# A three-stage kernel: the first stage's on-chip pools in another order, two pool ends aligned, and the stage's last stores issued by GpSimd

## The chip, the cores and the metric

The kernel runs on one core of one Trainium2 chip. The metric is the device time of one execution in microseconds (us). Before the change the median of three runs is 4724.49 us (4724.1 to 4726.25).

## What is computed

The reference is a forward pass and its gradients. With `x` of 2048 rows by 640 columns:

```python
xn = layernorm(x)
s  = A(xn, mem0, Wq, Wk, Wv, Wo)   # 64 segments of 32 rows, 32 heads of 128; 8 memory rows are carried on
g  = silu(B(xn, w1, w3, w2))       # B: (silu(xn w1) * (xn w3)) w2, hidden width 1728
out = x + s * g
# and the gradients of x, mem0, Wq, Wk, Wv, Wo, w1, w3, w2 for a given grad_out
```

Branch A is recurrent: each segment attends over 8 memory rows and its own 32 rows, and the first 8 rows of its result are the next segment's memory. Branch B is a gated feed-forward layer without recurrence. All tensors are bf16.

## The kernel before, in words

The work runs as a row of stages. Each stage opens its own tile pools in on-chip memory (SBUF) and in the matmul result banks (PSUM). Pools are laid out one behind the other in the order in which they are opened, and when a stage closes its pools the next stage's pools take the same addresses. The first instruction that touches a tile of a new pool waits until the old pools that this new pool overlaps have been left: by the engines that read or wrote their tiles, and by the transfers out of them.

**Stage one** (`phase12_ln_Bfwd`, L1809) normalizes the rows of `x`, stores them to the scratch tensor `XN`, and runs branch B forward in four blocks of 512 rows (`hidden`, L1868; `up`, L1900). It opens four SBUF pools in the order `bw` (the weights w1s, w3s, w2s, 52,480 bytes of a partition), `bio` (`hBT` and `xnT_b`), `bwork` (temporaries, among them `gb`, `dz`, `gs`), `ln` (the row tiles `xt0` to `xt7`). At its end (L1991 to L1999) it projects the first 672 rows of `XN` with Wv: 20 units of `first_rows` (L357) and one `last_rows` (L374), with the last block's four `up` calls in between, in units n = 1, 4, 7 and 10. A `first_rows` unit is ten matmuls in two halves; DVE copies the first half out of PSUM and ACT the second (L90, L92), into staging tiles `b0st` that take turns in the eight slots `xt0` to `xt7`, and each half is stored to the scratch tensor `QVX` by a DMA that SyncE (SP) issues (L371, L386): 42 stores in all.

**Stage two** (`phase3_Afwd`, L389) opens pool `W4` with Wq and Wo, pool `ast` with kT0, kT1, vt, hx0, hx1 and smaller tiles, and then calls `first_part` (L412). This opens `b0` (the turned rows `b0x`, and `ride0` and `kr0`) and `b0s` (four staging tiles of 1024 columns). Its work on the engines is: SP loads `b0x` as six turned blocks of 112 rows out of `XN` and then `ride0` (L270, called from L422 and L449); GpSimd (POOL) clears hx0 and hx1 (L427) and copies `ride0` into hx0 (L450). PE turns six heads of Wv (L444, called from L465), with each result copied into a ring in kT1 and stored to `WVT` by SP (L447). Then 42 units run (L468 to L495): `first_rows` and `last_rows` for Wk, then for Wq. ACT's queue issues the nine loads of Wq and Wo between them (L472), POOL stores the units up to n = 35 (to `KX` and `QVX`) and SP the rest.

**The recurrence** (`recurrence`, L555) opens `achain` and `afill` where `b0` and `b0s` lay and runs `chain(t)` (L598) 64 times. One step starts with two half projections by Wk, whose results DVE copies to the tile `stg` (L606); the next half, by Wq, goes into the bank that the first copy must have emptied. SP issues the step's stores and loads in the order in which they stand, `ride` (L572) among them.

The order within each engine's queue is the order in which instructions stand in the built program; `in_order` (L273) ties them. An instruction that waits holds back all that stand behind it on its engine.

In bytes of a partition, the old layout puts `bw` at 99,200 to 151,680, `bio` at 151,680 to 190,592, `bwork` at 190,592 to 218,880 and `ln` at 218,880 to 229,248. Stage two puts Wq and Wo at 99,200 to 181,120, `ast` at 181,120 to 211,456, `b0` at 211,456 to 220,224 and `b0s` from 220,224 on. The recurrence puts `achain` at 211,456 to 220,384.

Of the kernel before, what the change touches and what calls it, by code (L numbers as in the profile page):

```python
# [9 lines left out]
BF16 = mybir.dt.bfloat16  # L10
# [6 lines left out]
P = 128  # L17
# [255 lines left out]
def in_order(k, start):  # L273

    tc = k.tc
    last = {}
    for ins in tc.nc.cur_bb.bb.instructions[start:]:
        p = last.get(ins.engine)
        if p is not None:
            tc.add_manual_dep(ins, p.name, mybir.DependencyInfo(mybir.DependencyClass.NoSync, mybir.DependencyReason.DATA),  # L280
                              reason="written order")
        last[ins.engine] = ins
# [18 lines left out]
def packed_half(k, bank, x, W, b):  # L301

    for dc in range(k.DC):
        for g in range(4):
            c0 = g * 1024 + b * 512
            k.nc.tensor.matmul(bank[32 * g:32 * g + 32, :], x[:, dc, :], W[:, dc, c0:c0 + 512],  # L306
                               start=(dc == 0), stop=(dc == k.DC - 1), tile_position=(0, 32 * g),
                               skip_group_check=True)
# [48 lines left out]
def first_rows(k, ps, stage, xs, off, W, dst, x0, cg, tag="b0pb", w=1024, q=None):  # L357

    nc = k.nc
    for b in range(2):  # L360
        c0 = cg * 1024 + b * 512
        if w == 512 or b == 0:
            st = stage()
        pb = ps.tile([P, 512], F32, name="b0pb", tag=tag if isinstance(tag, str) else tag[b])
        for dc in range(k.DC):
            nc.tensor.matmul(pb[:], xs[:, dc, x0 - off:x0 - off + P], W[:, dc, c0:c0 + 512],
                             start=(dc == 0), stop=(dc == k.DC - 1))
        s0 = b * 512 if w == 1024 else 0
        k.copy(st[:, s0:s0 + 512], pb[:], eng='vs'[b])
        if w == 512 or b == 1:  # L370
            (q or nc.sync).dma_start(dst[x0:x0 + P, cg * 1024 + (b * 512 if w == 512 else 0):cg * 1024 + b * 512 + 512], st[:])  # L371


def last_rows(k, ps, stage, xs, off, W, dst, tag="b0pb", w=1024, q=None):  # L374

    x0 = k.NB0 - 32
    for b in range(2):
        if w == 512 or b == 0:
            st = stage()
        pb = ps.tile([P, 512], F32, name="b0pb", tag=tag if isinstance(tag, str) else tag[b])  # L380
        packed_half(k, pb, xs[:, :, x0 - off:x0 - off + 32], W, b)
        s0 = b * 512 if w == 1024 else 0
        k.copy(st[:, s0:s0 + 512], pb[:], eng='vs'[b])
        if w == 512 or b == 1:
            c0, c1 = (b * 512 if w == 512 else 0), b * 512 + 512
            (q or k.nc.sync).dma_start(dst[x0:k.NB0].rearrange("r (g c) -> g r c", g=4)[:, :, c0:c1], st[:])  # L386


def phase3_Afwd(k, W0, W4, Wv, Wk_, out2):  # L389
    nc, tc = k.nc, k.tc  # L390
    D, DC, S, H, HD, T = k.D, k.DC, k.S, k.H, k.HD, k.T
    Wq = W4.tile([P, DC, HD], BF16, name="Wq", tag="w2")
    Wo = W4.tile([P, H, D], BF16, name="Wo", tag="w3")
    with tc.tile_pool(name="ast", bufs=1) as st:
        kTs = [st.tile([P, H, 120], BF16, name=f"kT{i}") for i in range(2)]

        vt = st.tile([P, HD // 2], BF16, name="vt")
        hxs = [st.tile([P, DC, 32], BF16, name=f"hx{i}") for i in range(2)]
        qTs = [st.tile([P, 4, P], BF16, name=f"xqT{i}") for i in range(3)]
        xPs = [st.tile([P, 4, P], BF16, name=f"xP{i}") for i in range(3)]  # L400
        PTs = [st.tile([P, 4, P], BF16, name=f"xPT{i}") for i in range(2)]
        oTm = st.tile([P, H, 32], BF16, name="oTm")
        first_part(k, Wv, Wk_, Wq, Wo, kTs, vt, hxs, qTs + xPs + PTs + [oTm])
        with tc.tile_pool(name="aps", bufs=1, space=bass.MemoryType.PSUM) as ps, \
                tc.tile_pool(name="apm", bufs=1, space=bass.MemoryType.PSUM) as psm:
            banks = [psm.tile([P, 512], F32, name=f"bank{i}") for i in range(3)]
            own = kTs, vt, hxs, qTs, xPs, PTs, oTm
            WT = recurrence(k, W0, W4, Wv, Wk_, Wq, Wo, own, ps, banks)
            phase4_Abwd(k, out2, W4, WT, own, ps, banks)


def first_part(k, Wv, Wk_, Wq, Wo, kTs, vt, hxs, rest):  # L412
    nc, tc = k.nc, k.tc
    DC, H, HD = k.DC, k.H, k.HD
    with tc.tile_pool(name="b0", bufs=1) as io, tc.tile_pool(name="b0s", bufs=4) as stp, \
# [1 line left out]
            tc.tile_pool(name="b0k", bufs=2, space=bass.MemoryType.PSUM) as pk, \  # L417
            tc.tile_pool(name="b0w", bufs=2, space=bass.MemoryType.PSUM) as pw:
        start = len(nc.cur_bb.bb.instructions)
        xs = io.tile([P, DC, k.NB0], BF16, name="b0x")  # L420
        for x0 in range(0, k.NB0, 112):
            turned_load(k, xs[:, :, x0:x0 + 112], k.XN[x0:x0 + 112, :])  # L422
        wq = k.A_Wq.rearrange("(dc p) h e -> p dc (h e)", p=P)
# [43 lines left out]
        n = 0  # L467
        for W, dst in ((Wk_, k.KX[:, :]), (Wq, k.QVX[:, 0])):  # L468
            for x0 in list(range(0, k.NB0 - 32, P)) + [None]:
                for cg in range(4 if x0 is not None else 1):  # L470
                    if n % 2 == 1 and fetch:
                        nc.scalar.dma_start(*fetch.pop(0))  # L472
                    stage = lambda: stp.tile([P, 1024], BF16, name="b0st", tag="b0st")
# [1335 lines left out]
def phase12_ln_Bfwd(k: K, Wv, Wk_):  # L1809
    nc, tc = k.nc, k.tc  # L1810
    D, DC, S, F, FC, NT = k.D, k.DC, k.S, k.F, k.FC, k.NT
    BLK = 512
    NBLK = S // BLK
    TB = BLK // P
    fszs = [min(P, F - fc * P) for fc in range(FC)]
    with tc.tile_pool(name="bw", bufs=1) as wp, tc.tile_pool(name="bio", bufs=2) as io, \
            tc.tile_pool(name="bwork", bufs=2) as wk, tc.tile_pool(name="ln", bufs=1) as ln, \
            tc.tile_pool(name="bps", bufs=2, space=bass.MemoryType.PSUM) as ps:
        start = len(nc.cur_bb.bb.instructions)
        w1s = wp.tile([P, DC, F], BF16, name="w1s")  # L1820
# [73 lines left out]
        def up_ld(blk, ti):  # L1894
            tt = TB * blk + ti
            Gt = wk.tile([P, D], BF16, name="Gt", tag="Gt")
            nc.sync.dma_start(Gt[:], k.G[tt * P:(tt + 1) * P, :])
            gts[tt] = Gt

        def up(blk, ti):  # L1900
            hBT = hBTs[blk % 2]
            tt = TB * blk + ti
            rows = slice(tt * P, (tt + 1) * P)
            pz = ps.tile([P, 2, 512], F32, name="pz", tag="pz")
            for i in range(2):
                for fc in range(FC):
                    nc.tensor.matmul(pz[:, i, 0:320], hBT[:, fc, ti * P:(ti + 1) * P],
                                     w2s[:, fc, 320 * i:320 * i + 320], start=(fc == 0), stop=(fc == FC - 1))
            halves = lambda t: t[:].rearrange("p (i c) -> p i c", i=2)
            sz = wk.tile([P, D], BF16, name="sz", tag="sz")  # L1910
            nc.scalar.activation(halves(sz), pz[:, :, 0:320], ACT.Sigmoid)
            gb = wk.tile([P, D], BF16, name="gb", tag="gb")
            nc.vector.tensor_tensor(halves(gb), pz[:, :, 0:320], halves(sz), ALU.mult)
            nc.gpsimd.dma_start(k.GB[rows, :], gb[:])
            dz = wk.tile([P, D], BF16, name="dz", tag="dz")
            nc.scalar.activation(halves(dz), pz[:, :, 0:320], ACT.Sigmoid, scale=-1.0)
            nc.vector.tensor_tensor(dz[:], dz[:], gb[:], ALU.mult)
            nc.vector.tensor_tensor(dz[:], sz[:], dz[:], ALU.add)
            nc.gpsimd.dma_start(k.DZ[rows, :], dz[:])
            gs = wk.tile([P, D], BF16, name="gs", tag="gs")  # L1920
            nc.vector.tensor_tensor(gs[:], gts.pop(tt)[:], gb[:], ALU.mult)
            nc.gpsimd.dma_start(k.GS[rows, :], gs[:])
# [58 lines left out]
        xb = io.tile([P, DC, BLK], BF16, name="xnT_b", tag="xnT_b")  # L1981
# [3 lines left out]
        xa, off = xnTs[NBLK], 0  # L1985
# [5 lines left out]
        for n, (x0, cg) in enumerate([(x0, cg) for x0 in range(0, k.NB0 - 32, P) for cg in range(4)]):  # L1991
            if n % 3 == 1 and n // 3 < TB:
                up(NBLK - 1, n // 3)
                if n < 6:
                    up_ld(NBLK - 1, n // 3 + 2)
            if x0 == BLK:
                xa, off = xb, BLK
            first_rows(k, ps, stage, xa, off, Wv, k.QVX[:, 1], x0, cg, tag=("pg", "pu"), w=512)
        last_rows(k, ps, stage, xb, BLK, Wv, k.QVX[:, 1], tag=("pg", "pu"), w=512)  # L1999
        in_order(k, start)  # L2000


# [191 lines left out]
def kernel(  # L2194
# [34 lines left out]
    with tc.tile_pool(name="W0", bufs=1) as W0:  # L2229
        Wv, Wk_ = [W0.tile([P, k.DC, k.HD], BF16, name=nm, tag=tag) for nm, tag in (("Wv", "w0"), ("Wk", "w1"))]  # L2230
        phase12_ln_Bfwd(k, Wv, Wk_)
        with tc.tile_pool(name="W4", bufs=1) as W4:
            phase3_Afwd(k, W0, W4, Wv, Wk_, out_2)
# [38 lines left out]
```

## Time and profile before

| what | value |
|---|---|
| median of three runs | 4724.49 us |
| profiled execution, its time | 4722.13 us |
| profiled execution, its span from first to last instruction | 4720.1 us |
| PE (matmuls) busy | 4476.3 us, 95% |
| DVE, ACT, POOL busy | 48%, 34%, 44% |
| mean granted PE clock | 0.985 of full |
| PE in the last 12 us of stage one (250 to 262 us) | busy 12.00 of 12.00 us |
| PE from 262 to 272 us | busy 2.66 of 10.00 us |
| PE from 376.0 to 384.3 us | busy 2.87 of 8.30 us |
| DMA engines from 276 to 340 us | 98% and 101% of their time in the two parts of it |

The profile tells for each engine what it did and when (the timeline), with idle time ahead of an instruction in square brackets and the name of what ended that idle time. The granted clock is the share of full speed that the matmul engine was allowed in that stretch. Times count from the start of the span. "SPq" or "ACTq" marks the queue of an engine issuing a DMA; the time beside it is the issue alone and not the transfer.

### The profile page before, as it was taken

To read this page: it belongs to the slowest core of one execution; us is meant where nothing else is said; L and a number is where in the kernel's file an instruction comes from. 1 tells how busy PE (TensorE), PEld (TensorE's weight loads), DVE (VectorE), ACT (ScalarE), POOL (GpSimd) and SP (SyncE) were. 2 spreads that over 40 slices of the span, in tenths; PEclk is the share of its full clock that TensorE was granted. 3 is DMA by queue.
4 is the path that set the end of the run, shared out by engine and by line. 5 is a ranking of instruction groups with operands and counts; after the bars stand their busy time and mean duration, and the time that the engine had idled before them with its cause. 6 is when DMAs were issued, how large, how long until landed. Compare 5 with 4: busy or idle time off the path is not lost. (4 is left out here: it accounts for less than half of the span.)

```text
span 4720.1 us, 160254 instructions
## 1 busy us (share of the span) xinstructions
PE 4476.3 (95%) x64504; PEld 2824.1 (60%) x64504; DVE 2244.0 (48%) x7156; ACT 1588.8 (34%) x4360; POOL 2093.8 (44%) x3514
## 2 busy tenths in 40 slices
PE   8998999999999888999999998999999999999999
PEld 4544555555555555666666665666567666666675
DVE  8734666666666534555555553343234332311460
ACT  5432555555544533333333332232223322200000
POOL 6522555555555423444444444454345533311340
PEclk9998999999999998999999998999999999999999
DMA  8773666666555678777777774754345543579673
GB/s 265 238 244 106 176 182 179 177 180 178 175 174 167 169 179 230 208 215 203 212 210 213 205 210 133 163 150 133 109 125 157 145 125 109 170 219 208 154 183 100
DMA packets 977976, 834.81 MB, mean 177 GB/s; under 512 B 518674, under 2 KB 859862, under 8 KB 975272
## 3 DMA queue, kind: packets, MB, share of 16 engines
q1 hardware_dynamic: 765871, 549.75, 42.5%
q0 software_dynamic: 129088, 226.29, 16.2%
q10 hardware_dynamic: 82275, 48.52, 4.0%
q8 instruction: 509, 8.34, 0.8%
q14 instruction: 233, 1.91, 0.2%
HBM read 472.66 MB, written 310.33 MB: 166 GB/s over the span
## 5 line engine op out<-in xcount | busy, mean ns | idle before, releaser
L1647 PE MATMUL wg<-gr,hr 128*128 128x512 bf16 x2400 | 521.7, 379 | 0.0
L1628 PE MATMUL g<-w,ghacc 128*128 128x320 bf16 x3072 | 460.3, 300 | 0.8
L1647 PEld LDWEIGHTS <-hr 128*128 128x128 bf16 x2400 | 234.1, 98 | 278.7
L306 PEld LDWEIGHTS <-hx 128*32 128x32 bf16 x10240 | 247.0, 96 | 233.8 <-issue 19.6
L1628 PEld LDWEIGHTS <-ghacc 128*128 128x128 bf16 x3072 | 288.7, 98 | 104.6 <-ACT ghacc L92 2.2
L90 DVE CAST wgo<-wg 128x512 bf16<-128x512 f32 x72 | 49.8, 692 | 471.2 <-PE wg L1647 471.2
L90 DVE CAST stg<-bank 128x512 bf16<-128x512 f32 x256 | 177.0, 692 | 164.0 <-PE bank L306 152.6
L880 POOL DMA_DIRECT2D OR<-xv x163 | 89.8, 551 | 361.0 <-ACT xv L92 334.7
L92 ACT COPY ghacc<-t6g 128x768 bf16<-128x768 bf16 (+1 forms) x176 | 137.2, 780 | 303.6 <-PE t6g L1610 302.6
L1593 POOL DMA_DIRECT2D GSP<-grs x48 | 25.7, 549 | 474.3 <-ACT grs L1585 473.2
L325 PEld LDWEIGHTS <-gkv 128*8 128x8 bf16 x8192 | 178.6, 87 | 83.6 <-issue 4.1
L1324 POOL DMA_DIRECT2D VTD<-gvT x176 | 129.8, 743 | 218.0 <-ACT gvT L1323 210.2
L812 ACT ACTIVATE xP<-xsp,xnm 120x120 bf16<-120x120 f32 (+1 forms) x540 | 186.6, 374 | 29.2 <-DVE xnm L794 29.2
L832 POOL TENSOR_TENSOR xP<-xP,xrz 120x480 bf16<-120x480 bf16 x163 | 161.3, 989 | 76.3 <-DVE xrz L831 47.0
L336 DVE TENSOR_TENSOR fsum<-bank,fup 64x160 bf16<-64x160 f32 x254 | 69.5, 311 | 261.4 <-ACT fup L334 258.8
L1634 DVE TENSOR_TENSOR ghacc<-ghacc,g 128x320 f32<-128x320 f32 x192 | 93.5, 487 | 209.4 <-PE g L1628 209.4
L92 ACT CAST wgo<-wg 128x512 bf16<-128x512 f32 x48 | 28.1, 586 | 479.8 <-PE wg L1647 406.9
L1371 POOL DMA_DIRECT2D GXP<-gks x157 | 91.5, 583 | 195.2 <-ACT gks L1369 193.0
L325 PE MATMUL bank<-Wo,oTm 128*32 128x320 bf16 x4032 | 154.6, 307 | 18.5 <-DVE oTm L684 18.5
L325 PE MATMUL bank<-WvT,gkv 128*8 128x320 bf16 x4096 | 170.2, 310 | 0.0
L306 PE MATMUL bank<-Wq,hx 128*32 128x512 bf16 x2560 | 163.0, 384 | 5.4 <-DVE stg L90 5.4
L325 PE MATMUL bank<-WkT,gkv 128*8 128x320 bf16 x4096 | 162.8, 299 | 4.2 <-issue 2.5
(390 smaller groups left out, 10944.1 us busy)
## 6 DMA issues: line engine op xcount, KB each, us to landing
QVS<-stg SPq DMA_DIRECT2D x128, 256.0 KB
kT<-VTD SPq DMA_DIRECT2D x64, 320.0 KB
PR<-xP POOLq DMA_DIRECT2D x168, 120.0 KB, 3.3
VTD<-gvT POOLq DMA_DIRECT2D x168, 120.0 KB, 4.1
dS<-DSR SPq DMA_DIRECT2D x168, 120.0 KB
P<-PR SPq DMA_DIRECT2D x168, 120.0 KB
OR<-xv POOLq DMA_DIRECT2D x163, 120.0 KB, 3.1
orr<-OR SPq DMA_DIRECT2D x14, 1280.0 KB
```

Of the source, the lines that this page charges most:

```text
L90: return nc.vector.tensor_copy(out, in_)
L92: return nc.scalar.copy(out, in_)
L306: k.nc.tensor.matmul(bank[32 * g:32 * g + 32, :], x[:, dc, :], W[:, dc, c0:c0 + 512], start=(dc == 0), stop=(dc == k.DC - 1), tile_positio ...
L325: k.nc.tensor.matmul(pm[p0:p0 + nq, 0:320], x[:, h, :], W[:, h, 320 * b:320 * b + 320], start=(first and i == 0), stop=(last and i == 15), ...
L812: nc.scalar.activation(Pb[0:n, j, 0:n], sp[0:n, j, :], ACT.Exp, bias=nmx[0:n, j:j + 1], scale=k.scale, accum_out=Z[0:n, j:j + 1])
L832: eng.tensor_tensor(Pb[0:n, :, 0:n], Pb[0:n, :, 0:n], bc_last(rz[0:n], n), ALU.mult)
L880: q.dma_start(k.OR[120 * tl:120 * tl + n, c0:c0 + 512], v[0:n])
L1324: nc.gpsimd.dma_start(k.VTD[tl][:, :, h0:h0 + 4, :], vTq[:])
L1371: (nc.sync if (tl, qd) in pro else nc.gpsimd).dma_start(k.GXP[tl, :, qd, 0:ns], ks[:].rearrange("p s i h m -> p s i (h m)"))
L1628: nc.tensor.matmul(pg[:], ring[:, i, j, r0:r0 + P], Ws[qd][i][:, j, 320 * h:320 * h + 320], start=(i == 0 and j == 0), stop=(i == 2 and j ...
L1634: nc.vector.tensor_tensor(a, a, pg[:], ALU.add)
L1647: nc.tensor.matmul(pw[:], hr[:, tl, dc * P:(dc + 1) * P], grs[i][:, tl, :], start=(tl == 0), stop=(tl == NF - 1))
```

## The change

Stage one opens its pools in the order `bio`, `bwork`, `ln`, `bw`. By the addresses of the built kernel `bio` now lies at 99,200 to 138,112, `bwork` to 166,400, `ln` to 176,768 and `bw` at 176,768 to 229,248. So `ast`, `b0` and `b0s` of stage two lie on the weights, and Wq and Wo on the other three pools. The tile `b0x` becomes 16 columns wider (160 bytes of a partition, never read), so that `b0` ends at 220,384, where `achain` ends. The staging stores of Wv from unit n = 14 on, twelve by L371 and the two of L386, are issued by POOL in place of SP.

```diff
@@ first_part
-        xs = io.tile([P, DC, k.NB0], BF16, name="b0x")
+        xs = io.tile([P, DC, k.NB0 + 16], BF16, name="b0x")
@@ phase12_ln_Bfwd
-    with tc.tile_pool(name="bw", bufs=1) as wp, tc.tile_pool(name="bio", bufs=2) as io, \
-            tc.tile_pool(name="bwork", bufs=2) as wk, tc.tile_pool(name="ln", bufs=1) as ln, \
+    with tc.tile_pool(name="bio", bufs=2) as io, tc.tile_pool(name="bwork", bufs=2) as wk, \
+            tc.tile_pool(name="ln", bufs=1) as ln, tc.tile_pool(name="bw", bufs=1) as wp, \
             tc.tile_pool(name="bps", bufs=2, space=bass.MemoryType.PSUM) as ps:
@@
-            first_rows(k, ps, stage, xa, off, Wv, k.QVX[:, 1], x0, cg, tag=("pg", "pu"), w=512)
-        last_rows(k, ps, stage, xb, BLK, Wv, k.QVX[:, 1], tag=("pg", "pu"), w=512)
+            first_rows(k, ps, stage, xa, off, Wv, k.QVX[:, 1], x0, cg, tag=("pg", "pu"), w=512, q=nc.gpsimd if n >= 14 else None)
+        last_rows(k, ps, stage, xb, BLK, Wv, k.QVX[:, 1], tag=("pg", "pu"), w=512, q=nc.gpsimd)
```

The built program shows what else moves. The rows of PE, DVE and ACT stand as before. On SP the six loads of `b0x` and the load of `ride0` now stand behind the twentieth store of Wv's projection and ahead of eight further ones (units 10 to 13). On POOL the clearing of hx0 and hx1, and the copy of `ride0` that waits for its load, now stand ahead of the fourteen stores that POOL takes over. On SP the recurrence's first `ride` load stands ahead of the last store of `first_part` in place of behind it.

What the first instructions wait for in the built program also changes. The first `b0x` load used to wait for the transfers out of `bwork` and `ln`, the last two Wv stores among them; now it waits for PE's last read of w2s, in the last `up`. The first load of Wq used to wait for none of these; now it waits for the stores of Wv's projection, the last two included. The first copy into `stg` used to wait for the last stores out of `b0s`; now it waits for the loads of `kr0` and the work on `b0`.

## The prediction

> **What bounds the kernel now.** The page comes first: PE is busy 95% of the span, so what counts is PE's idle time and time at a low clock. The chain of waits covers only the last 7% of the span and does not reach the changed stages. So I read PE's timeline from 255 us, where stage one ends, to 425 us, where the second loop step ends, and looked up what ended each idle time.
>
> ```profile
> PE 4476.3 (95%) x64504; PEld 2824.1 (60%) x64504; DVE 2244.0 (48%) x7156; ACT 1588.8 (34%) x4360; POOL 2093.8 (44%) x3514
> ```
> ```profile
> 259.72 2.34 PE L306 MATMUL b0pb<-Wv,xnT_b 128*32 128x512 bf16 x40
> 262.79 0.72 PE L444 MATMUL wpt<-ident,Wv 128*128 128x128 bf16 x10 [0.73 <-ACT b0st L92]
> 264.13 0.72 PE L444 MATMUL wpt<-ident,Wv 128*128 128x128 bf16 x10 [0.62 <-ACT kT L92]
> 265.35 0.72 PE L444 MATMUL wpt<-ident,Wv 128*128 128x128 bf16 x10 [0.50 <-ACT kT L92]
> 271.56 4.00 PE L366 MATMUL b0pb<-Wk,b0x 128*128 128x512 bf16 x10 [5.48 <-DMA b0x<-XN]
> ...
> 275.67 2.32 PE L366 MATMUL b0pb<-Wk,b0x 128*128 128x512 bf16 x10
> ```
>
> Columns are start, duration, engine, line. Two things are to be seen: PE stands for 5.48 us until `b0x` is there, and the ten matmuls after it take 4.00 us where the next ten take 2.32. The clock says why (columns: PE busy, clock, DMA share, GB/s):
>
> ```profile
> 267.00:268.00 1.00, 0.00 (x0) 1.00 0.00 0
> 268.00:269.00 1.00, 0.00 (x0) 0.58 0.34 78
> ...
> 274.00:275.00 1.00, 1.00 (x4) 0.51 0.57 120
> 275.00:276.00 1.00, 1.00 (x10) 1.00 0.66 141
> ```
>
> SP's timeline gives the cause: the last Wv store is issued at 262.8 to 263.3 us and the first `b0x` load not before 267.22, when that store had landed, 3.9 us after its issue.
>
> ```profile
> 261.75 1.56 SPq L386 DMA_DIRECT2D QVX<-b0st  x2
> 267.22 7.80 SPq L270 DMA_TRANSPOSE b0x<-XN  x6
> 275.07 1.27 SPq L270 DMA_TRANSPOSE ride<-XN  x1
> ```
>
> The second hole is in the first loop step, on PE and on DVE, again behind a store:
>
> ```profile
> 376.51 2.33 PE L306 MATMUL bank<-Wk,hx 128*32 128x512 bf16 x40
> 384.27 2.32 PE L306 MATMUL bank<-Wq,hx 128*32 128x512 bf16 x20 [5.43 <-DVE stg L90]
> ```
> ```profile
> 383.53 1.29 DVE L90 CAST stg<-bank 128x512 bf16<-128x512 f32 x2 [7.12 <-DMA QVX<-b0st]
> ```
>
> **First hole.** In the new layout `b0x` lies on w2s, whose last reader is the last `up` (PE, over at 237.9 us). The seven turned loads then run on SP from about 237.95 to 247.0 (7.80 + 1.27 us of issue) and the last has landed by 249 (`ride0` was issued until 276.34, and POOL's copy of it started at 278.20: 1.9 us). They are in place 17 us before PE asks, so the 5.48 us go. PE comes from the six turns of Wv at 266.07 (0.7 us of idle at most between them, clock still 1.00), so the cold start goes too: the unit took 275.67 - 271.56 = 4.11 us against 278.11 - 275.67 = 2.44 warm, 1.67 us. What is late next is the six turns themselves, with 0.73, 0.62 and 0.50 us that wait for ACT and stay.
>
> **Stores of KX.** PE loses 0.50 and 0.78 us more, at 287 and 293 us, to copies that wait for KX stores. POOL issued the first one at 278.72, held back by the `ride0` copy (over at 278.5), while its data were there at 276.2, and it took 7.7 us to land beside the weight loads. Now that copy is done at 249.4, and the first store leaves at 269.0, before the first load of Wq (269.7). Its slot is wanted at 276.9; even 7.7 us make 276.7. Between 0 and 1.28 us; I take all of it, as each later store keeps a margin through the four PSUM banks.
>
> **What it costs: SP's queue.** The eight stores of units 10 to 13 stand behind the seven loads, with 9.1 us of issue. The first of them, ready at 242.3, goes out at 247.05. No row shows the landing of such a store when eight are queued; from below 2.0 us (GB, POOL's quickest), from above 7.7 us (KX under full DMA); the nearest row is the last Wv store, the same 1 KB rows at the same light DMA load: 3.9 us after 0.5 us of issue, 4.4. So it lands at 251.45. Its slot is wanted by unit 14's DVE copy at 247.96, which ends at 252.15 instead. Behind it on DVE stand the copies of the next units; PE has two banks for this half and asks for it again in unit 16, at 250.7. Cost 252.15 - 250.7 = 1.45 us, nothing if the landing is below 3 us. The other seven follow 0.33 us apart, faster than copies come (1.08 us), so it is paid once.
>
> **What it costs: POOL's queue.** The two memsets (0.41 us) pass the last `up`'s stores and wait for PE at 237.9, ahead of `gb` at 239.8: nothing. The `ride0` copy blocks POOL until 249.4; behind it stands unit 14's store, which is ready only at 248.4 to 252.2: nothing. Then 14 stores come every 1.08 us. An issue costs POOL 0.54 us (min/median/max 540/542/569 ns for the KX stores with DVE's casts running beside them), and landing takes 2.0 to 3.6 us: the slots are back in 4.1 us, wanted after 8 x 1.08 = 8.6. Here a rule of the Trainium skill speaks against the change: "SBUF — State Buffer", section "SBUF: two separate sides", says that GpSimd cannot write a DMA's descriptors while DVE is in a two-port mode, which copies and casts can enter, and its part "A bandwidth-pool intuition that's wrong" gives 3.1 us in place of 0.62 for such a DMA. By the rule the 14 stores need 43 us and end at 252.2 + 43.4 = 295.6; by the row they keep pace and end at 263.3. I take the row, since the casts are the same form on the same engine.
>
> **The new wait of Wq.** The first Wq load on ACT's queue now waits for all Wv stores. Behind it stand ACT's copies, and PE behind those. ACT reaches it at 266.07 + 2.3 + 0.6 + 0.7 = 269.7 us; the last POOL store goes out at 263.3 and lands by 266.9. The 1.45 us above moves both. The margin is 2.8 us; if it is gone, PE's banks hide some 4.9 us more.
>
> **Second hole.** `achain` now overlaps `b0` alone, and the first `stg` copy waits for the last `kr0` load (issued by 371.4 before) and reads of `b0x`, not for the store. The step then runs as the next one does: from the start of the Wk half to L647 it took 390.98 - 376.51 = 14.47 us, and the next step 411.44 - 403.64 = 7.80, less 0.27 for a `kr` turn that step 0 does not have: 7.53. Gain 6.94 us, of which 5.43 are idle and 1.5 cold clock. The `ride` load ahead of the last store costs SP 1.25 us, and the wait for that store now falls on the first `kr` load: store out at 378.65, landed 5.6 us after its issue (from the row above) at 384.8. A `kr0` load issued at 338.52, under full DMA, was there at 342.64, 4.1 us; so `kr` is there by 388.9, and PE wants it at 396.45 - 6.94 = 389.5. Hidden, by 0.6 us or more. Behind `kr` on SP stands only the v store, ready at 384.8. The gap of 1.79 us for ACT's table load stays.
>
> **Sum.** 5.48 + 1.67 + 1.28 + 6.94 - 1.45 = 13.9 us. The recurrence is a serial chain and PE goes on from there, so an earlier start is an earlier end. 4722.13 - 13.9 = 4708.2 for the profiled execution; the median lies 2.36 above it, so **4710.6**. Bounds of the open terms: the SP stall 0 to 4.7, KX 0 to 1.28, a 1.65 us wait for `kr0` at 342 us that may go or double.
>
> **Rivals.**
> (a) The hole moves to the stores. If the eight SP stores land in 7.7 us, unit 14's copy ends at 247.05 + 7.7 + 0.69 = 255.4, 4.7 late; the POOL store behind it returns its slot at 255.4 + 0.54 + 7.7 = 263.7, wanted at 256.6 + 4.7 = 261.3, 2.4 more. That is 7.1 in place of 1.45: 4716.3. For it: KX's median. Against it: DMA share 0.36 there, 0.98 at KX.
> (b) The change does not do what it says: some wait on an old store stays in front of both holes, 4724. The built program's waits speak against it.
> (c) Slower, by the rule above: POOL's stores end at 295.6 and land at 297.6. ACT stands at the Wq load from 271.1 (269.7 + 1.45), less 4.9 us of banks: 21.6 us, so 4732. It decides from 2.55 us a store on ((271.1 + 4.9 + 13.9 - 2.0 - 252.2) / 14). Against it: 0.54.
> (d) A bonus. Loop steps 0 to 2 run their 64 output matmuls in 4.33, 4.37 and 4.46 us against 2.36 in step 3, at clock 0.50. If a shifted start leaves them warm, 6.1 us more: 4704.5.
>
> **How the numbers follow.** Forecast 0.70 (own range 4706 to 4714), (a) 0.13, (b) 0.07, (c) 0.04, (d) 0.06. The range 4705 to 4717.5 leaves out (b), (c), and the tails of (a) and (d). About 0.2% (9.4 us) is what a measurement can tell from no change: faster 0.70 + 0.06 + 0.03 of (a), same 0.17, slower 0.04.
>
> **What would show it.** Right: the first L366 on `b0x` starts within 0.2 us of the last Wv turn and takes 2.3 us; the first `stg` copy has no idle time behind a DMA; both at clock 1.00. A DVE or ACT copy in units 14 to 16 that waits for a QVX store gives the cost. Wrong: an ACT copy idle before the first Wq issue, POOL DMA issues above 1 us, or a new PE wait on `kr` or `vt` in step 0.

## The result and the profile after

| | before | after |
|---|---|---|
| median of six executions each, same chip | 4724.03 us (4716.35 to 4726.25) | 4703.28 us (4700.42 to 4706.63) |
| ratio after to before, 95% interval | | 0.9956 [0.9945, 0.9968] |
| profiled execution (its span) | 4722.13 us (4720.1) | 4705.37 us (4703.7) |

By this comparison the kernel is 20.75 us faster, 15.1 to 26 us with the interval. The forecast was 4710.6, with a range of 4705.0 to 4717.5: the sign is right, and the median lies 1.7 us below the range. The profiles differ by 16.8 us.

The page's first line hardly moves (PE busy 4474.1 us, 95%), since the changed stretches are 3% of the span.

**The first hole is gone.** PE's timeline of the kernel after, at the same place as the first one shown of before:

```profile
266.11 0.72 PE L444 MATMUL wpt<-ident,Wv 128*128 128x128 bf16 x10 [0.50 <-ACT kT L92]
266.67 2.32 PE L366 MATMUL b0pb<-Wk,b0x 128*128 128x512 bf16 x10
```

The first ten matmuls on `b0x` follow the last Wv turn with no bracket, and take 2.32 us in place of 4.00. The clock in one-microsecond windows (PE busy, clock, DMA share, GB/s, as before) is 1.00 in all eight from 262 to 270 us; two of them:

```profile
266.00:267.00 1.00, 0.89 (x12) 0.75 (x12) 0.27 (x2) 0.47 (x2) 0.00 (x0) 1.00 0.77 233
267.00:268.00 1.00, 1.00 (x7) 0.42 (x5) 0.41 (x2) 0.28 (x1) 0.00 (x0) 1.00 1.02 365
```

SP's timeline of the kernel after shows the loads right behind the last `up`, and the eight stores that now stand behind them:

```profile
238.79 7.79 SPq L270 DMA_TRANSPOSE b0x<-XN  x6
246.62 1.26 SPq L270 DMA_TRANSPOSE ride<-XN  x1
247.99 3.95 SPq L371 DMA_DIRECT2D QVX<-b0st  x8
```

**The second hole is gone, and another wait has come.** PE's timeline of the first loop step after the change:

```profile
369.51 2.33 PE L306 MATMUL bank<-Wk,hx 128*32 128x512 bf16 x40
371.67 1.25 PE L306 MATMUL bank<-Wq,hx 128*32 128x512 bf16 x20
...
376.91 0.96 PE L647 MATMUL bank<-qmT,kT 128*40 128x8 bf16 x32
379.51 0.24 PE L657 MATMUL bank<-ident,sTm 40*128 40x40 bf16 x2 [1.63 <-ACT sTm L649]
...
383.03 0.30 PE L674 MATMUL bank<-ident,Pm 128*40 128x128 bf16 x2 [2.73 <-DVE Pm L669]
...
385.78 4.24 PE L325 MATMUL bank<-Wo,oTm 128*32 128x320 bf16 x64
```

The Wq half starts with no wait. But PE idles 1.63 us at L657 and 2.73 us at L674, where before it was 0.46 and 1.79, and the 64 output matmuls still run at half clock. The same rows of before:

```profile
392.40 0.21 PE L657 MATMUL bank<-ident,sTm 40*128 40x40 bf16 x2 [0.46 <-ACT sTm L649]
...
394.72 0.30 PE L674 MATMUL bank<-ident,Pm 128*40 128x128 bf16 x2 [1.79 <-DVE Pm L669]
...
397.20 4.33 PE L325 MATMUL bank<-Wo,oTm 128*32 128x320 bf16 x64
```

ACT's timeline of the kernel after has the reason:

```profile
378.13 1.07 ACT L92 CAST stg<-bank 128x512 bf16<-128x512 f32 x2 [7.76 <-DMA QVS<-stg]
```

ACT's copy of the V half waits for a staging slot to be stored. SP's timeline around it:

```profile
371.07 0.66 SPq L386 DMA_DIRECT2D QVX<-b0st  x1
372.62 0.34 SPq L612 DMA_DIRECT2D KS<-stg  x1
```

`stg` has two slots. The V half takes the one that the Wk half filled, and in the built program its copy waits for the store of that slot to `KS`, not for the `QVS` store that the row names (in one later run the row names `KS`). That store was issued at 372.62 and the copy ran at 378.13, 5.5 us later.

### The profile page after: what moved, and what is told of

It is laid out like the page before. It is cut to its first block, busy times and chain, and to the rows that moved or that the text cites. A ratio compares the mean times of both kernels' runs of the same rounds, so it can differ in the third digit from the quotient of the medians.

```text
span 4703.7 us, 160233 instructions
## 1 busy us (share of the span) xinstructions
PE 4474.1 (95%) x64504; PEld 2824.8 (60%) x64504; DVE 2245.5 (48%) x7156; ACT 1587.4 (34%) x4360; POOL 2097.9 (45%) x3528
## 5 line engine op out<-in xcount | busy, mean ns | idle before, releaser
L1324 POOL DMA_DIRECT2D VTD<-gvT x176 | 129.5, 741 | 216.0 <-ACT gvT L1323 206.4
L325 PE MATMUL bank<-Wo,oTm 128*32 128x320 bf16 x4032 | 154.7, 308 | 18.5 <-DVE oTm L684 18.4
L245 POOL DMA_DIRECT2D r<-GOS x256 | 145.6, 574 | 36.4 <-issue 9.5
```

Of the source, the lines that this page charges most:

```text
L245: eng.dma_start(d, src if src.shape[0] > 1 else src[0])
L325: k.nc.tensor.matmul(pm[p0:p0 + nq, 0:320], x[:, h, :], W[:, h, 320 * b:320 * b + 320], start=(first and i == 0), stop=(last and i == 15), ...
L1324: nc.gpsimd.dma_start(k.VTD[tl][:, :, h0:h0 + 4, :], vTq[:])
```

## The experiments

Each group of kernels ran on one chip beside the kernel before: e1 to e4 on one, e5 to e8 on a second, e9 and e10 on a third. Two theories stood at the start. The first: the sum of about 14 us is what the change is worth, and the other 7 us of the first comparison are the chance of single executions. The rival: the change does something further out, worth 7 us more each time.

### The same two kernels again

No edit: `e1_before_again` is the kernel before, `e2_after_again` the kernel after.

> The kernel before, once more, unaltered. Theory of chance: executions differ by which later stretches happen to run at half clock and by how long transfers take, so this profile differs from the first one of before by several us between 465 us and the end (about 5 us either way), while the stretch from 238 to 465 us, with its two holes, repeats within 2 us (227 us). Ratio to before within 0.1% of 1. Rival, a systematic surplus: the stretch from 2000 to 2250 us repeats within 2 us of the 250.0 us of the first profile, so that the 10 us that the changed kernel saves there come from the change.

> The changed kernel, once more, unaltered. Theory of chance: the stretch from the last up call to the start of the recurrence's fourth step again takes about 15 us less than before (14 to 16), and the timed gain over five rounds is 14 to 20 us, nearer to the 15 than the 20.75 of the first comparison; the stretch from 2000 to 2250 us of before differs between the two profiles of this kernel by several us. Rival, a systematic surplus: the gain stays at 20 to 21 us and the later stretch again is about 10 us shorter than in both profiles of before.

Measured: the kernel before against itself is 1.0006 [0.9997, 1.0016], with medians of 4722.9 us (12 executions) and 4719.98 us (30). The 30 executions reach from 4710.43 to 4728.33. The kernel after is 0.9972 [0.9961, 0.9983], 4705.76 us (11 executions). On another chip the kernel after ran once more:

> The changed kernel for the third time. Theory of chance: over five more rounds the gain is 11 to 17 us (0.23% to 0.36%), and the stretch from 2000 to 2300 us of before is again between 280 and 293 us. Rival, a systematic surplus: the gain is 20 us or more.

Measured: 0.9972 [0.9961, 0.9982], 4710.41 us (12 executions, 4703.92 to 4727.14) against 4726.02 (21, 4714.24 to 4735.05).

The two ratios, from 23 executions of the kernel after, say a gain of 13 us, with intervals from 8 to 18.4; the first comparison, from six, says at least 15.1. A gain of 20 or more is outside both later intervals, so the rival in that size falls. All three agree from 15.1 to 18.4 us. Two details were missed: the stretch that e1 was to repeat within 2 us came out 3.1 us shorter, and e2 took 12.7 us less up to the fourth loop step where 14 to 16 were expected.

Where chance enters is seen by stretches of the span that hold the same work (end points taken by a DVE instruction that both kernels have). The three columns of each kernel are its three profiles, of before only two:

| work that lies in before at | before | before again | after | after again | after, third |
|---|---|---|---|---|---|
| 240 to 467 us (all that the diff touches) | 226.9 | 223.8 | 211.9 | 214.4 | 220.3 |
| 600 to 2009 us | 1408.6 | 1412.9 | 1408.4 | 1405.8 | 1406.0 |
| 2009 to 2300 us | 291.4 | 289.5 | 280.7 | 279.9 | 284.6 |
| 4303 to 4502 us | 199.2 | 200.5 | 204.6 | 203.5 | 201.2 |

Stretches that the diff does not touch move by 1 to 5 us between profiles of one kernel, and by 5 to 12 us over all five. In the stretch from 2009 us the kernel before spent 17.1 us at half clock in one profile and 10.2 in the next, the kernel after 3.4, 0 and 6.8. Half clock comes in pieces of 3.41 us and whole multiples of it, and which pieces are hit differs in part from one execution to the next. All three profiles of after are shorter there and longer in the stretch from 4303 us. The seven variants below also take 277 to 285 us in the stretch from 2009 us, so it is shorter in all ten profiles with an edit. But from 467 us to the end these ten take 4243.9 to 4258.1 us and the two of before 4252.9 and 4256.7 us: most of what that stretch saves is lost elsewhere. The means differ by 3.3 us, within the spread, so a lean of the later work on the shifted start is not shown.

### Each part alone

`e3_align_only` is the kernel before with the wider tile alone, `e7_no_align` the kernel after without it, `e4_sp_stores` the kernel after with all stores on SP:

```diff
 e3 (on before)
-        xs = io.tile([P, DC, k.NB0], BF16, name="b0x")
+        xs = io.tile([P, DC, k.NB0 + 16], BF16, name="b0x")
 e7 (on after)
-        xs = io.tile([P, DC, k.NB0 + 16], BF16, name="b0x")
+        xs = io.tile([P, DC, k.NB0], BF16, name="b0x")
 e4 (on after)
-            first_rows(..., q=nc.gpsimd if n >= 14 else None)
-        last_rows(..., q=nc.gpsimd)
+            first_rows(...)
+        last_rows(...)
```

> The kernel before with the 16 columns added to b0x and nothing else. Theory that the two holes are separate: the first hole stays (5.5 us of idle at b0x and ten matmuls in 4.0 us), the second goes, with no DVE wait behind QVX at the first stg copy; step 0 takes 22 to 23 us in place of 27.1, so a gain of 4.5 us, 0.1%. Rival, that the stg wait needs the new pool order as well: step 0 stays at 27 us and the time does not move.

> The changed kernel without the 16 columns: the new pool order and the GpSimd stores alone. Theory that the holes are separate: the first hole is gone as in the changed kernel (first b0x matmul within 0.2 us of the Wv turns, at full clock), the second is back (a DVE wait of about 7 us behind QVX at the first stg copy, 5.4 us of PE idle), and step 0 takes 27 us. So the time lies about 4.5 us above the changed kernel and 9 us below the kernel before, 0.19%. Rival, that the pool order alone already helps the first loop step: step 0 stays at 22.6 us.

> The changed kernel with the last 14 Wv stores left on SP. Theory that POOL's part is worth nothing: SP issues a store in 0.33 us and copies come every 1.08, the stores land by 266 us as before, the first b0x matmul still follows the Wv turns within 0.2 us, and the time is within 0.1% of the changed kernel. Rival, that POOL's part is needed: stores behind the turned loads on SP fall behind, units 14 to 18 wait for slots or the first Wq load holds ACT, and the time is 2 to 7 us above the changed kernel.

Measured: e3 0.9993 [0.9985, 1.0002], 4715.14 us (11); e7 0.9975 [0.9965, 0.9985], 4714.21 (9); e4 0.9971 [0.996, 0.9982], 4707.1 (8); e3 and e4 against the 4719.98, e7 against the 4726.02.

In PE's timeline e3 keeps the first hole, whole:

```profile
265.83 0.72 PE L444 MATMUL wpt<-ident,Wv 128*128 128x128 bf16 x10 [0.50 <-ACT kT L92]
272.39 4.04 PE L366 MATMUL b0pb<-Wk,b0x 128*128 128x512 bf16 x9 [5.84 <-DMA b0x<-XN]
```

and e7 keeps the second:

```profile
368.23 2.33 PE L306 MATMUL bank<-Wk,hx 128*32 128x512 bf16 x40
375.90 2.32 PE L306 MATMUL bank<-Wq,hx 128*32 128x512 bf16 x20 [5.34 <-DVE stg L90]
```

So the pool order removes the first hole and the 16 columns the second, each by itself. The first loop step, from its Wk half to the next one, takes 27.1 us before (26.8 to its last copy into hx), 27.2 in e7, 22.5 in e3 and 22.6 after. The two parts are then worth some 12 and 3 us by the timed ratios, and the 3 is not told from zero. By the traces they are worth about 7 us (idle time and cold start) and 4.6 us (the step).

GpSimd's share shows no worth: with the stores on SP the ratio is 0.9971 against 0.9972, and the step and the first hole are as in the kernel after. Each ratio has an interval of about 5 us to either side, so a us or two would not be seen.

### What holds the KS store up

The theory after these runs: the `KS` store lands late because the 256 KB store of L386 is ahead of it on SP's queue. `e5_last_by_pool` sends that store by GpSimd:

```diff
-                    last_rows(k, ps, stage, xs, 0, W, dst, q=nc.gpsimd if n < 36 else nc.sync)
+                    last_rows(k, ps, stage, xs, 0, W, dst, q=nc.gpsimd)
```

> The changed kernel with one store moved: the last store of the first part (256 KB of QVX, L386) is issued by GpSimd in place of SP. Theory that in step 0 ACT's copy of the V half waits for the KS store because that store lands late behind the 256 KB store on SP: the KS store, issued at the same place, lands within 3.3 us as in step 1, ACT copies at once, PE's idle time in step 0 falls by 1.1 us at the sTm transposes and by about 1 us at the Pm transposes, and step 0 takes 20 to 20.6 us in place of 22.6. Rival, that the KS store is late for another cause (its form, or the transfers as a whole): it again takes 5.1 to 5.2 us from the end of its issue and step 0 stays at 22 to 23 us. The timed gain over the changed kernel, 2 us, is below what the rounds tell apart.

Measured: 0.9958 [0.9945, 0.9971], 4705.04 us (5), but the wait is there. SP issued the `KS` store at 377.22 and ACT's timeline has

```profile
382.64 1.07 ACT L92 CAST stg<-bank 128x512 bf16<-128x512 f32 x2 [7.67 <-DMA QVS<-stg]
```

5.4 us after the issue. The step took 22.5 us. The theory of the queue falls. The records of single packets show another thing. Of the first sixteen packets of the L386 store eight take 0.35 to 0.94 us in the kernel after, where later packets of the same 2 KB mostly take 0.08. It is the same in the kernel before (0.36 to 0.94 us), where no other store runs beside it. When GpSimd issues the store, in packets of 4 KB, the first eight take 0.31 to 1.57 us and later ones mostly 0.16. The theory from this: whatever comes next waits behind those packets, on whichever queue it stands. Then the store must come earlier, not elsewhere. `e9_last_earlier` (on the kernel after) moves the unit of the last rows for Wq ahead of the four units that stood before it, so that its store leaves some 10 us sooner:

```diff
-            for x0 in list(range(0, k.NB0 - 32, P)) + [None]:
+            for x0 in ((0, 128, 256, 384, None, 512) if W is Wq else (0, 128, 256, 384, 512, None)):
```

> The changed kernel with the 32-row unit of Wq (last_rows) put ahead of Wq's last four units, so that its 256 KB store (L386) is issued some 9 us before step 0. Theory that this store's own packets, which take 0.6 to 1.2 us each at first where others take 0.09, occupy the DMA engines that the KS store needs, whichever queue issues it: the KS store of step 0 now lands within 3.3 us of its issue, ACT copies the V half without a wait, PE idle falls from 1.6 to 0.5 us at the sTm transposes and from 2.7 to 3.3 to about 2 us at the Pm transposes, and step 0 takes 19.8 to 20.4 us in place of 21.9 to 22.3. Rival, that the KS store is late because it is the first store into KS or stands behind the turned load of ride: it again takes 5 us and step 0 stays near 22 us.

Measured: 0.9964 [0.9952, 0.9976], 4709.24 us (5) against 4725.66 (11). The timelines of SP, ACT and PE in e9:

```profile
363.19 0.67 SPq L386 DMA_DIRECT2D QVX<-b0st  x1
...
374.51 0.52 SPq L371 DMA_DIRECT2D QVX<-b0st  x1
376.17 0.32 SPq L612 DMA_DIRECT2D KS<-stg  x1
```
```profile
379.15 0.59 ACT L92 CAST stg<-bank 128x512 bf16<-128x512 f32 x1 [5.35 <-PE bank L306]
```
```profile
370.62 0.34 PE L461 MATMUL kpt<-ident,kr 96*128 96x96 bf16 x4 [1.39 <-DMA kr<-KX]
...
381.89 0.21 PE L657 MATMUL bank<-ident,sTm 40*128 40x40 bf16 x2 [0.46 <-ACT sTm L649]
...
384.22 0.30 PE L674 MATMUL bank<-ident,Pm 128*40 128x128 bf16 x2 [2.11 <-DVE Pm L669]
```

The L386 store now leaves 13 us ahead of `KS`, and ACT's copy waits for PE alone. PE's wait at L657 is 0.46 again, as before the change, and the step takes 393.32 - 373.06 = 20.3 us in place of 22.6. A store of the other form (L371), of the same 256 KB, now leaves 1.7 us ahead of `KS` and holds nothing up, so it is not the size. The slow packets are where the L386 store is (364.5 to 365.5 us, means of 0.35 and 0.81), and a `kr` load issued 2.7 us behind that store is now late: 1.39 us at L461. So the L386 store itself, and not its queue, holds up what follows; that it does so by its slow packets fits all of this, but no run changed the packets alone. Why packets of this form (four groups of 32 rows) start so slowly was not tried and stays open. Of the 2.3 us the `kr` wait takes 1.4 back, and in the time of the whole kernel nothing of it can be seen.

### The cold output matmuls

Steps 0 to 2 run their 64 output matmuls mostly at half clock, after (4.24, 4.46 and 2.93 us) as before (4.33, 4.37, 4.46); little of the bonus (d) of the prediction came. In the second profile of before they take 3.41, 4.01 and 2.99 us, so differences of this size come without a change. The theory: the clock drops because PE idles around L657 and L674. `e6_warm` (on e5) gives PE four more filler matmuls there in steps 0 to 2, whose results nothing reads; `e10_earlier_warm` is e9 with the same edit:

```diff
-                    for i in range(WARM.get(g, 0)):
+                    for i in range(WARM.get(g, 0) + (4 if g == "G2" and t < 3 else 0)):
```

> The same, with four more filling matmuls (whose result nobody reads) while PE waits for the Pm transposes in loop steps 0, 1 and 2. Theory that steps 0 to 2 run their 64 output matmuls at half clock because PE has too little work in the window before: the clock stays at 1.00 in steps 0 to 2, the output matmuls take 2.4 us in place of 4.2 to 4.5, and the three steps take about 2 us less each: 18.3 to 18.7 us, some 6 us in all, so 0.1% below the kernel without them. Rival, that the half clock has another cause than the idle time: the output matmuls stay at 4.2 us and more, and the added matmuls cost nothing or some tenths of a us.

> The same, with the four more filling matmuls ahead of the Pm transposes in steps 0, 1 and 2. If the theory of the slow store holds, step 0 now also has little idle time and may stay at full clock: output matmuls 2.4 us in steps 0 to 2, step 0 near 18 us, steps 1 and 2 at 17.4 to 17.7 us. The time is about 8 us below the changed kernel, near 0.9955 of before. Rival: step 0 stays at half clock because of its table load, as it did with the filling matmuls alone (4.46 us); then 6 us below the changed kernel.

Measured: e6 0.9943 [0.993, 0.9957], 4697.53 us (5); e10 0.9937 [0.9924, 0.9951], 4697.01 us (6). In e6 the output matmuls take 4.46, 2.36 and 2.36 us in steps 0 to 2: step 0, where PE stands 2.45 us at L657 behind the `KS` store, stays cold. In e10, where that stall is gone, all three take 2.36:

```profile
381.80 1.03 PE L915 MATMUL bank<-Wq,ident 128*128 128x512 bf16 x4 [0.16 <-issue]
...
385.73 2.36 PE L325 MATMUL bank<-Wo,oTm 128*32 128x320 bf16 x64
```

The granted clock of e10 ahead of them (window, then PE busy and the other engines; the third number from the end is the clock):

```profile
380.00:384.00 4.00, 2.46 (x45) 1.57 (x43) 2.54 (x9) 2.51 (x4) 1.56 (x4) 1.00 0.35 114
```

and of the kernel after, taken again, over the same work:

```profile
378.00:382.00 4.00, 0.70 (x5) 0.38 (x7) 2.88 (x9) 1.61 (x3) 1.55 (x4) 0.88 0.18 66
382.00:386.00 4.00, 3.78 (x70) 2.19 (x72) 0.92 (x3) 0.38 (x2) 0.23 (x1) 0.50 0.31 91
```

With PE busy 0.70 of 4 us the next stretch is granted half; with 2.46 of 4 it is not. That is one pair and no threshold: among all windows of 3.41 us in the profile of before, some with PE busy 73% were followed by half clock and some with less than 50% were not. The fillers show that PE's lack of work is the cause in these steps: with them the clock stays at 1.00 in five steps of six.

Steps 0 to 3 of e10 take 17.6, 17.4, 17.4 and 17.6 us from one Wk half to the next; after, 22.6, 20.3, 18.7 and 17.6. That is 9.1 us. e10 is 30 us (24 to 36) faster than the kernel before: it beats both kernels. That is more than expected (0.9955 lies outside its interval), and more than the 17 to 20 us that its profile saves up to 467 us against the two of before; the rest is not explained.

## Why the prediction came out as it did

Step by step, by its own terms:

| step | predicted | profile after |
|---|---|---|
| first hole, idle | -5.48 | -5.48 |
| first hole, cold start | -1.67 | -1.67 (a unit takes 2.44 us) |
| stores of KX | -1.28 | about -0.2 (in e8 +2.4) |
| stall by SP's eight stores | +1.45 | 0 |
| first loop step | -6.94 | -4.52 |
| sum | -13.9 | -11.9 |

From PE's start on the work behind the last `up` to the second loop step, the time went from 403.64 - 237.76 = 165.88 us to 392.12 - 238.60 = 153.52, 12.4 less; small gaps outside the rows make the other 0.5 us. In the two later profiles of after it is 153.4 and 157.6 us.

**First hole: right**, in cause and size.

**SP's stores: the term was mis-sized.** The mechanism came: DVE waits for the store of its slot, but less long than said.

```profile
250.12 0.69 DVE L90 CAST b0st<-b0pb 128x512 bf16<-128x512 f32 x1 [2.79 <-DMA QVX<-b0st]
```

The store was issued from 247.99 on, so it was back 2.1 us later, not 4.4, and the prediction itself had put the cost at nothing below 3 us. PE runs through without a break. The row taken as nearest was the last Wv store: the same 1 KB rows, but the L386 form. In the trace of before the 256 packets of its two stores come slowly, from 263.0 to 266.6 us, at most 48 in half a microsecond; the eight L371 stores after move 124 to 133 in each. POOL's light stores, whose 2.0 us the prediction took as its lower bound, were nearer. Rival (a) falls with it.

**POOL's stores: right.** They keep pace, with DVE's copies running beside them:

```profile
251.11 1.60 POOL L371 DMA_DIRECT2D QVX<-b0st  x3 [1.36 <-DVE b0st L90]
```

An L371 issue costs 0.54 us as in the row of before, not the 3.1 us that rival (c) took for each store from the Trainium skill ("SBUF — State Buffer", part "A bandwidth-pool intuition that's wrong"). The section lets casts into the two-port mode only "when their operands meet the conditions", and the prediction did not ask whether these casts out of PSUM do. So the run shows no such wait beside these casts, and does not contradict the page. The last issue ends at 264.6; the forecast was 263.3, in a profile whose stretch began 0.84 us earlier. The first Wq load left ACT at 269.81 (forecast 269.7) without a wait. Rival (c) falls; so does (b), and (d) in the main.

**KX: given back.** The 0.50 and 0.78 us are gone at their places, but PE waits 0.39 and 0.22 us for copies further on, and 2.11 in place of 1.65 us for `kr`:

```profile
328.39 2.32 PE L366 MATMUL b0pb<-Wq,b0x 128*128 128x512 bf16 x10 [0.39 <-DVE b0st L90]
...
335.63 0.34 PE L461 MATMUL kpt<-ident,kr 96*128 96x96 bf16 x4 [2.11 <-DMA kr<-KX]
```

That is 1.28 - 1.07. The DMA engines are full there (98% and 101% of their time before), so taking all of the 1.28 was too much. In all, PE's waits between the first `b0x` matmul and the loop are 2.9 us before, and 2.7, 2.8 and 5.3 us in the three profiles of after. That an earlier arrival only waits later when the transfers set the pace fits these, but is argued.

**First loop step: right up to L647, then too much.** From the Wk half to L647 it took 376.91 - 369.51 = 7.40 us (forecast 7.53, before 14.47). From there on the prediction left the step at its old pace (403.64 - 390.98 = 12.66 us), and this failed: 392.12 - 376.91 = 15.21 us, 2.55 lost. The waits of 1.63 and 2.73 us in place of 0.46 and 1.79 make 2.11 of them. The question "what is late next" was asked for `kr` and `vt`, but not for the slot of `stg`. In the kernel before, the removed hole lay between the L386 store and the `KS` store:

```profile
377.40 0.56 SPq L386 DMA_DIRECT2D QVX<-b0st  x1
...
384.85 0.48 SPq L612 DMA_DIRECT2D KS<-stg  x1
```

They left 7.4 us apart, and in the kernel after 1.6 us. The hole, which was the wait for that very store, had covered its slow packets. e9 shows that without that store in the way 2.3 us come back.

**From the span to the median: where it failed.** The forecast of 4710.6 was 4708.2 for the profiled execution and 2.36 us more for the median, as in the three executions of before. The profiled execution came at 4705.37, 2.8 us below. Its terms gave 12.4 us and not 13.9. But the loop from its second step to the point at 467 us took 60.9 us in place of 63.6, and the second profile of before takes 60.6 without any change, so this is chance; the work further out made the other 1.7 us. The median then lay 2.09 us below its profiled execution, not 2.36 above: 4.45 us more. That is the step that failed: the offset was the chance of three executions, which lay 2 us apart, and the prediction gave the spread of executions no room in its range, though it put what a measurement can tell from no change at 9.4 us. Thirty executions of the kernel before on one chip lie 18 us apart, and 11 of the kernel after beside them reach from 4693.54 to 4719.89. A range worked out from the bounds of the steps, 12.5 us wide, was too narrow for a median of six.

The 7.3 us by which the first median lies below the forecast come from no term of the sum: the terms give 8 to 12 us in the three profiles of after, and the two later comparisons 13. Their medians, 4705.76 and 4710.41, lie within the range, but beside medians of before that differ by 6 us between the chips, so the closeness of the second to 4710.6 is luck. What made up the rest of the 7.3 us beyond chance, if anything, is not settled; the later intervals allow the sum and up to 4.5 us more.

## What to carry to other kernels

A wait for the space of a pool costs its idle time and then the cold clock after it; which pool a new one lands on can be chosen, here for 7 us by the trace, at no price that shows. Before removing a stall, list each buffer and each store that the stall had given time: one of them is late next, and a store is best compared with a row of the same form. And see the spread of many executions before setting a range from three.

## What the runs showed of the hardware

- One form of store (L386, 256 KB) has packets of 0.3 to 0.99 us among its first sixteen on SP's queue, and up to 1.57 us on GpSimd's, where later ones mostly take 0.08 and 0.16; another queue does not help, an earlier issue does. A store that left 1.5 to 2 us after it landed 5 us or more after its issue (after, e5), a light one of the L371 form within 2.1 us.
- Half clock came and went on one grid of 3.41 us in each execution: 139.8 and 145.1 us of it in the two profiles of before, which are equally long (4720.1 us), and 138.1, 129.5 and 142.9 us in the three of after. Two long pieces (23.9 and 17 to 20 us) stand at the same work in each of these, most short ones do not. How much of the spread between executions this makes is not shown.
- Four filler matmuls (1.03 us in all) ahead of the output matmuls took these from 4.2 to 4.5 us to 2.36 us (steps 0 and 1 of e9 and e10).
